# One reading transfer per tile, an earlier place for four pieces of the weights, and three groups of sums on GpSimd in a Fourier mixing and ELU kernel

## The chip, the cores and the metric

The kernel runs on one core of one Trainium2 chip. The metric is the device time of a whole execution in microseconds; the time before is the median of 3 runs. The core has a matrix engine (TensorE, PE in the profile, its weight loads PEld), a vector engine (VectorE, DVE), an activation engine (ScalarE, ACT), GpSimd (POOL) and SyncE (SP), which here only issues transfers. Each engine runs its own queue strictly in the order of the program; engines wait for one another through semaphores.

## The reference

```python
# x: (8, 3008, 256); filt_r, filt_i: (1505, 256), float32; w_in: (256, 2048); w_out: (2048, 256), float64
X = np.fft.rfft(x, axis=1)
y = np.fft.irfft(X * (filt_r + 1j * filt_i)[None], n=3008, axis=1).astype(np.float32)
h = y.reshape(24064, 256) @ w_in
g = np.where(h > 0, h, np.exp(np.minimum(h, 0)) - 1.0)
out = (g @ w_out).astype(np.float32)
```

The weights arrive as 8-byte floats (`moe_w_in`, `moe_w_out` are read as pairs of 32-bit words) and have to be turned into 4-byte floats on the core.

## The kernel before, in words

**Three factors of the Fourier step.** A sequence of 3008 = 47 x 64 rows is transformed by three small matrix factors. The first factor works on rows 47 apart (`a_first` for the first batch, `a_unit` for the other seven). The second factor, with the filter's product and the way back, goes over groups g of four frequencies (`b_first`, `products`, `bi_first` for batch 0; `b_unit`, `re_mult`, `im_mult`, `bi_unit` for the others). Its result goes to a DRAM buffer `yds[b]` of 32 x 96 rows of 256 floats (`y_write_first`, `y_write`). The third factor (`n_unit`) reads it back in six parts m: `y_read` brings a tile of 128 partitions x 4 rows (512 KB), and `n_unit` multiplies it with a table `tn` of 128 x 128 per row, which yields the transposed input y of the two large products. The partition p*32+k of that tile holds part p (0 to 3) of frequency k (0 to 31), so one read is four transfers of 32 partitions; the first read (`y_read_first`) is eight, because the last four frequencies are written last and are read apart.

**The two large products.** For each of the 48 tiles (b, m) there are four quads q, each a seven-product Strassen form of `y @ w_in` (ups, with the tiles phs, pha, phd in PSUM), the ELU, and the seven products with `w_out` (downs, tiles po). The item i runs the ups of quad i and the downs of quad i-1, so quad q of the first tile needs `w_in[q]`, and one quad later `w_out[q]`. `n_sums` makes the three combinations of y which the seven products need. In the first tile a seven-product step is 4 matmuls of 224 columns, in the later ones of 256 columns.

**The weights.** `w_in` and `w_out` are cut into 16 pieces k = 4q + j: pieces with j = 0, 1 are the two halves of `w_in[q]`, those with j = 2, 3 the two halves of `w_out[q]`. Each piece goes through `w_fetch` (a transfer of 512 KB), `w_split` (two operations on VectorE), `w_float` (four on ScalarE, parts 0 to 3), `w_join` (on VectorE: sign and exponent, mantissa sum, then the product that lands in `w_in[q]` or `w_out[q]`), and after the second piece of a pair `w_sums` (four additions of 128 x 256 floats on VectorE, for the combined weights of the seven products). Six sets of temporaries (`wtmp`) hold pieces between split and join.

**The order.** The program is written out by hand (`tc.manual_schedule`). A boot part does the first factor of batch 0, pieces 0 to 6, then the loop over g of the second factor (lines 868 to 883) with some floats in between (`floats`), then the first read, pieces 7 to 13 in part, seven idle matmuls (`warm`), and `n_unit(0, 0)`. After it comes the loop over items (line 976). In it a table `plan` holds what else is issued in a quad, under (quad, place): place 2 is behind the third of the quad's first seven or eight steps, place 0 behind all of these, place 1 at the quad's end. In the first quads the plan has the rest of the weights and the start of batch 1: `x_unit` and `a_unit` in quads 2, 3 and 4 (they also issue `x_load` and `z_write`), `f_pairs` in quads 1 to 4 (DRAM to DRAM transfers for the filter), `z_read` in quad 5 and `b_unit` in quad 6. SyncE issues nearly all transfers, in program order, and waits in that order too.

The lines in question: `y_read` 472, `y_read_first` 477, `w_split` 709, `w_float` 715, `w_join` 724, `w_sums` 745, the loop of the second factor 865 to 883, the boot's end 884 to 897, the plan's list 920 to 925, the items 976 to 998. In the profile the additions of `w_sums` have lines 749 to 752, the operations of `w_join` 728, 730 and 735 or 741, those of `w_split` 712 and 713, of `w_float` 722; 627 is a down product, 545 an up product, 494 the third factor's, 233 the first factor's of batch 1.

Of the kernel before, what the change touches and what calls it, by code (L numbers as in the profile page):

```python
# [11 lines left out]
FP32 = mybir.dt.float32  # L12
U32 = mybir.dt.uint32
AXT = mybir.ActivationFunctionType
ALU = mybir.AluOpType
# [11 lines left out]
P = 128  # L27
D = 256
B = 8
DFF = 2048  # L30
H = 24
K2 = 32
# [9 lines left out]
def _make_tables():  # L42

    n2, k2 = np.arange(N2), np.arange(K2)
    ta, tn = np.zeros((P, H, P)), np.zeros((P, H, P))
    for i in range(H):
        for h in range(2):
            if h and i == 0:
                continue  # L60
            n1 = N1 - i if h else i
            th = 2 * np.pi * (((N1 * n2[:, None] + n1) * k2[None]) % N) / N
            c, s = np.cos(th), -np.sin(th)
            c[:, 0], s[:, 0] = 1.0, 1.0 - 2.0 * (n2 % 2)
# [12 lines left out]
    c, s = np.cos(th), np.sin(th)  # L77
    sign = np.where(q < 24, 1.0, -1.0)
    gb[0:24, 0, :N1], gb[24:48, 0, :N1] = c, s
    gb[64:88, 0, :N1], gb[88:112, 0, :N1] = c * sign, -s * sign  # L80
    for o in (0, 64):
        gr[o:o + N1, 0, 0:24], gr[o:o + N1, 0, 24:48] = 2 / N * c.T, 2 / N * s.T
        gi[o:o + N1, 0, 0:24], gi[o:o + N1, 0, 24:48] = 2 / N * (c * sign).T, -2 / N * (s * sign).T
    k1 = np.arange(24)[None]
    t0 = 2 * np.pi * ((i * k1) % N1) / N1
    t3 = 2 * np.pi * ((i * (32 + 64 * k1)) % N) / N
    c0, s0, c3, s3 = np.cos(t0), np.sin(t0), np.cos(t3), np.sin(t3)
    gb[0:24, 1, 0:24], gb[24:48, 1, 24:48] = c0, c3
    gb[64:88, 1, 24:48], gb[88:112, 1, 0:24] = -s3, -s0

    m0, m3 = np.full((24, 1), 2 / N), np.full((24, 1), 2 / N)
    m0[0] = m3[23] = 1 / N
    s0[:, 0] = s3[:, 23] = 0.0
    gr[0:24, 1, 0:24], gr[24:48, 1, 24:48] = m0 * c0.T, m3 * c3.T
    gi[0:24, 1, 24:48], gi[24:48, 1, 0:24] = -m0 * s0.T, -m3 * s3.T

    fb, bb = np.zeros((P, 2, 32)), np.zeros((P, 2, 4, 32))
    for p in range(4):  # L100
        r = slice(32 * p, 32 * p + 24)
        fb[r, 0, :24] = (-1.0 if p == 3 else 1.0) * gb[24 * (p % 2):24 * (p % 2) + 24, 0, 0:24]
        q = (0, 24, 64, 88)[p]
        k = 24 if p in (1, 2) else 0
        fb[r, 1, :24] = gb[q:q + 24, 1, k:k + 24]
    for o in range(0, P, 32):
        for p, (t, c) in enumerate(((gr, 0), (gr, 24), (gi, 0), (gi, 24))):
            bb[o:o + 24, 0, p, :24] = t[0:24, 0, c:c + 24]

    bb[0:24, 1, 0, :24], bb[0:24, 1, 1, :24] = gr[0:24, 1, 0:24], gr[24:48, 1, 24:48]  # L110
    bb[0:24, 1, 2, :24], bb[0:24, 1, 3, :24] = gi[24:48, 1, 0:24], gi[0:24, 1, 24:48]
    pairs = np.concatenate([fb.reshape(P, 64), bb.reshape(P, 2 * P)], 1)
    lie = np.concatenate([2 * np.arange(24), 2 * np.arange(24) + 1])
    gb[:, :, lie] = gb[:, :, :48].copy()
    for t in (gr, gi):
        for o in (0, 64):
            t[o + lie] = t[o:o + 48].copy()
    gf = np.zeros_like(gb)
    for o in (0, 64):
        gf[o:o + 48] = gb[o:o + 48].reshape(2, H, 2, 64).swapaxes(0, 1).reshape(48, 2, 64)  # L120
    once = np.stack([np.eye(P), gf.reshape(P, P)], 1)
    return [t.astype(np.float32) for t in (ta, tn, np.stack([gb, gr, gi], 1), tf, once, pairs)]

# [7 lines left out]
def kernel(  # L131
# [9 lines left out]
    nc = tc.nc  # L141
# [18 lines left out]
    t4p = pool("t4p", 2)  # L160
# [308 lines left out]
        w = tns[b, m] = tnp.tile([P, 4, P], FP32, tag="tn", name="tn")  # L469
        nc.sync.dma_start(w, tn_d[:, 4 * m:4 * m + 4, :])  # L470

    def y_read(b, m, queues=(nc.sync, nc.sync)):
        t = t4s[b, m] = t4p.tile([P, 4, D], FP32, tag="t4", name="t4")
        for p in range(4):
            queues[p % 2].dma_start(t[p * 32:p * 32 + 32, :, :], yds[b][:, p * H + 4 * m:p * H + 4 * m + 4, :])

    def y_read_first():
        t = t4s[0, 0] = t4p.tile([P, 4, D], FP32, tag="t4", name="t4")
        for k in (slice(0, K2 - 4), slice(K2 - 4, K2)):
            for p in range(4):  # L480
                nc.sync.dma_start(t[p * 32 + k.start:p * 32 + k.stop, :, :], yds[0][k, p * H:p * H + 4, :])

    def half(m):

# [197 lines left out]
    wds = {}  # L682
# [24 lines left out]
    wts, wtmp = {}, []  # L707

    def w_split(k):
        m, e, f, l = wts[k] = wtmp[{9: 2, 12: 3, 13: 4, 15: 5}.get(k, k % 2)]  # L710
        hi = wds[k][:, :, 1]
        nc.vector.tensor_scalar(out=m, in0=hi, scalar1=0x000FFFFF, scalar2=None, op0=ALU.bitwise_and)
        nc.vector.tensor_scalar(out=e, in0=hi, scalar1=0x7FF00000, scalar2=None, op0=ALU.bitwise_and)
# [7 lines left out]
            o, x, func, scale, bias = steps[i]  # L721
            nc.scalar.activation(out=o, in_=x, func=func, scale=scale, bias=bias)  # L722

    def w_join(k):
        q, j = divmod(k, 4)
        m, e, f, l = wts.pop(k)
        hi = wds.pop(k)[:, :, 1]
        nc.vector.scalar_tensor_tensor(out=e, in0=hi, scalar=0x80000000, in1=e,
                                       op0=ALU.bitwise_and, op1=ALU.bitwise_or)
        nc.vector.tensor_tensor(out=f, in0=f, in1=l, op=ALU.add)  # L730
        e = e.bitcast(FP32)
        if j < 2:
            f, e = (t.rearrange("p (a j c) -> p a j c", a=2, j=2) for t in (f, e))
# [8 lines left out]
        if j % 2 == 1 and k < 7:  # L742
            w_sums(k)

    def w_sums(k):
        q, j = divmod(k, 4)
        w = (w_in if j < 2 else w_out)[q]
        a11, a21, a12, a22, s1, s2, s4 = (w[:, i] for i in range(7))
        nc.vector.tensor_tensor(out=s1, in0=a21, in1=a22, op=ALU.add)
        nc.vector.tensor_tensor(out=s2, in0=s1, in1=a11, op=ALU.subtract)  # L750
        nc.vector.tensor_tensor(out=s4, in0=a12, in1=s2, op=ALU.subtract)
        nc.vector.tensor_tensor(out=a21, in0=a11, in1=a21, op=ALU.subtract)

    def f_arrange():

# [27 lines left out]
    with tc.manual_schedule():  # L783


        with tc.tile_pool(name="boot", bufs=1) as bp:
# [75 lines left out]
            w_split(7)  # L862
            w_join(6)
            w_split(8)
            floats = {0: (7, 0, 1), 1: (7, 2, 3), 4: (8, 0, 1), 5: (8, 2, 3), 6: (9, 0, 1), 7: (9, 2, 3)}
            for g in range(4):
                t_first(g)
            for g in range(NG + 2):
# [10 lines left out]
                    w_float(*floats[g])  # L879
                if g == 1:  # L880
                    w_split(9)
                if 3 <= g < 6:
                    w_fetch(g + 8, nc.sync)
            y_read_first()
            for k in (14, 15):
                w_fetch(k, nc.sync)
            for k in (7, 8):
                w_join(k)
                w_split(18 - k)
                w_float(18 - k)  # L890
            for k in (12, 13):
                w_split(k)
                w_float(k)
            w_sums(7)
            w_join(9)
            w_sums(9)
            w_join(10)
            warm = psO.tile([P, 512], FP32, tag="po2", name="warm")
            for k in range(7):
                nc.tensor.matmul(warm, w_in[0][:, 0, 0, :], w_in[0][:, 0:2].rearrange("p a b c -> p (a b c)"),  # L900
# [15 lines left out]
        def at(quad, place, fn, *a):  # L916
            plan.setdefault((quad, place), []).append((fn, a))


        for quad, place, fn, *a in ((0, 0, w_split, 14), (1, 2, w_join, 11), (1, 2, w_split, 15), (1, 2, w_float, 14, 0, 1),  # L920
                                    (1, 1, w_float, 14, 2), (2, 2, w_sums, 11), (2, 2, w_float, 14, 3),
                                    (2, 2, w_float, 15, 0), (2, 1, w_join, 13), (2, 1, w_sums, 13), (2, 1, w_float, 15, 1),
                                    (3, 2, w_float, 15, 2, 3), (3, 1, w_join, 14), (3, 1, w_join, 15),
                                    (4, 2, w_sums, 15)):
            at(quad, place, fn, *a)
        for c in range(2, XBUFS):
            at(c - 2, 0, x_load, 1, c)
# [6 lines left out]
        for b in range(B):  # L934
# [28 lines left out]
            for m, (s, place) in enumerate(((23, 0), (25, 1), (29, 1), (32, 0), (36, 0), (40, 0))):  # L963
# [4 lines left out]

                    at(*((t + s + 1, 1) if m > 2 else (t + s, place)), n_sums, b, m)
                if b == 0 and m == 1:  # L970
                    at(1, 1, w_join, 12)
                at(t + PER + 4 * m + 5, 0, c_unit, b, m)
                at(t + PER + 4 * m + 6, 0, o_unit, b, m)

# [1 line left out]
        for i in range(-PER, len(items) + 3):  # L976
# [3 lines left out]
            for n, k in enumerate("DUUDUDDU" if i in opens else "UUDUDDU"):  # L980
                s = ups if k == "U" else downs
                if s:
                    s.pop(0)()
                if n == 2:
                    for fn, a in plan.get((i, 2), ()):
                        fn(*a)
            for fn, a in plan.get((i, 0), ()):
                fn(*a)
# [42 lines left out]
```

## Time and profile before

| | us |
|---|---|
| median of 3 runs | 2598.8 (2598.58 to 2601.48) |
| the profiled execution | 2598.4 |
| its span | 2596.6 |
| TensorE busy in the span | 2549.5 |
| VectorE busy | 2042.1 |
| ScalarE busy | 1548.0 |
| GpSimd busy | 159.0 |
| mean granted clock of TensorE, as a share of full speed | 0.995 |

The profile is of one execution. Its time is 1.8 us over its span, for what lies ahead of the first and behind the last instruction. Starts are in us from the span's start. In a timeline a row gives start, duration, engine, line, operation, operands and shape, a count, and in brackets how long the engine sat idle before it and what released it. A busy share says little of the path: what counts is where TensorE, which is busy nearly all the time, stands still, and which wait ends last there. Transfers that are issued by SyncE show when they are issued, and seldom when they land. A transfer's tile can bear the name of another tensor that shares its memory: the wait of the third factor at 84.5 us is said to be for `t<-in_moe_w_out_dram`, and the program has `y_read_first` there.

### The profile page before, as it was taken

How to read it: one execution, taken by the hardware profiler on the slowest of the kernel's cores; microseconds unless marked ns; L12 is line 12 of the kernel's file. 1: busy time of each engine (PE TensorE's matmuls, PEld its weight loads, DVE VectorE, ACT ScalarE, POOL GpSimd, SP SyncE). 2: the span in 40 equal slices, each digit the busy share in tenths (PEclk: the TensorE clock that was granted, in tenths of full speed). 3: DMA queues.
4: the chain of work that ended last, by engine and by line, in shares of the span. 5: the costliest groups of instructions: out<-in, count | busy, mean ns of one | idle time of the engine just before them, and what ended most of it. 6: DMA issues, size and time to landing. Idle time of an engine off the chain costs nothing.

```text
span 2596.6 us, 39712 instructions
## 1 busy us (share of the span) xinstructions
PE 2549.5 (98%) x14474; PEld 2203.3 (85%) x14474; DVE 2042.1 (79%) x3536; ACT 1548.0 (60%) x2713; POOL 159.0 (6%) x313
## 2 busy tenths in 40 slices
PE   6889999999999999999999999999999999999998
PEld 4778889888898888988889888888889888898887
DVE  6968887788877888788886888778887788866666
ACT  6755655666556655665566655566555655555554
POOL 4000100010000000000000000000000011000000
PEclk9999999999999999999999999999999999999999
DMA  9663213522234231433215231343213322110010
GB/s 286 180 162 76 70 27 94 130 70 58 52 91 119 60 76 47 116 82 76 63 41 146 70 84 37 78 121 85 59 44 85 91 59 69 43 43 20 21 29 17
DMA packets 231475, 206.37 MB, mean 79 GB/s; under 512 B 130962, under 2 KB 197714, under 8 KB 231280
## 3 DMA queue, kind: packets, MB, share of 16 engines
q1 hardware_dynamic: 215920, 172.95, 27.1%
q0 software_dynamic: 14000, 30.44, 4.2%
q8 instruction: 114, 1.87, 0.3%
q10 hardware_dynamic: 1360, 0.46, 0.1%
q14 instruction: 81, 0.66, 0.1%
HBM read 131.87 MB, written 78.17 MB: 81 GB/s over the span
## 4 chain that ended last, share of the span: by engine, by line
PE 96%; DMA 2%; DVE 1%; ACT 1%; issue 0%; SPq 0%; DVEq 0%; ACTq 0%
PE po L627 44%; PE phs L545 25%; PE phd L545 12%; PE pha L545 6%; PE psn L494 3%; PE psa L233 1%; PE pf L382 1%; PE pv L454 1%; DMA t<-in_moe_w_in_dram 1%; DMA wd<-in_moe_w_out_dram 0%; DMA xc<-in_x_dram 0%; DMA yd<-t 0%; PE po L295 0%; PE po L329 0%; PE psr L329 0%
## 5 line engine op out<-in xcount | busy, mean ns | idle before, releaser
L627 PE MATMUL po<-g,wo 128*128 128x256 f32 (+1 forms) x5376 | 1314.7, 376 | 6.9 <-DVE wo L741 4.8
L627 PEld LDWEIGHTS po<-g,wo 128*128 128x128 f32 x5376 | 1012.9, 190 | 171.1 <-issue 49.4
L556 ACT ACTIVATE g<-phs 128x512 f32<-128x512 f32 (+1 forms) x576 | 339.0, 589 | 762.2 <-PE phs L545 760.8
L563 ACT ACTIVATE e<-e 128x512 f32<-128x512 f32 (+1 forms) x768 | 477.2, 621 | 24.4
L553 DVE TENSOR_TENSOR g<-phd,g 128x512 f32<-128x512 f32 (+1 forms) x384 | 259.4, 676 | 295.1 <-ACT e L563 204.1
L545 PE MATMUL phs<-ys,wi 128*128 128x256 f32 (+1 forms) x1536 | 388.5, 375 | 1.5 <-ACT g L556 1.5
L545 PE MATMUL phs<-y,wi 128*128 128x256 f32 (+1 forms) x1536 | 388.6, 375 | 0.0
L567 DVE SCALAR_TENSOR_TENSOR g<-e,g 128x512 f32<-128x512 f32 (+1 forms) x576 | 387.0, 672 | 0.3 <-ACT e L563 0.2
L562 ACT ACTIVATE e<-g 128x512 f32<-128x512 f32 (+1 forms) x576 | 353.4, 614 | 44.3 <-DVE g L553 37.1
L545 PEld LDWEIGHTS phs<-ys,wi 128*128 128x128 f32 x1536 | 292.0, 190 | 35.5 <-ACT g L556 2.2
L545 PEld LDWEIGHTS phs<-y,wi 128*128 128x128 f32 x1536 | 288.2, 190 | 36.1 <-ACT r L387 0.4
L567 DVE SCALAR_TENSOR_TENSOR g<-e,phs 128x512 f32<-128x512 f32 (+1 forms) x192 | 129.8, 676 | 141.3 <-ACT e L563 140.9
L545 PE MATMUL phd<-ys,wi 128*128 128x256 f32 (+1 forms) x768 | 195.3, 377 | 1.7 <-DVE g L553 1.7
L545 PE MATMUL pha<-y,wi 128*128 128x256 f32 (+1 forms) x768 | 194.4, 376 | 1.2 <-ACT t L722 1.2
L545 PE MATMUL phd<-y,wi 128*128 128x256 f32 (+1 forms) x768 | 193.7, 375 | 0.0
L562 ACT ACTIVATE e<-phs 128x512 f32<-128x512 f32 (+1 forms) x192 | 113.0, 589 | 128.8 <-PE phs L545 128.8
L545 PEld LDWEIGHTS phd<-ys,wi 128*128 128x128 f32 x768 | 144.5, 190 | 22.6 <-DVE g L553 6.8
L545 PEld LDWEIGHTS pha<-y,wi 128*128 128x128 f32 x768 | 145.5, 191 | 19.2 <-ACT t L722 1.5
L545 PEld LDWEIGHTS phd<-y,wi 128*128 128x128 f32 x768 | 145.8, 190 | 16.5
L323 POOL DMA_DIRECT2D fall<-fp x224 | 110.4, 501 | 732.2 <-DVE r L427 704.5
L553 DVE TENSOR_TENSOR g<-pha,g 128x512 f32<-128x512 f32 (+1 forms) x192 | 129.1, 672 | 27.0 <-PE pha L545 26.9
L607 DVE TENSOR_TENSOR g<-g,g 128x512 f32<-128x512 f32 (+1 forms) x192 | 130.7, 681 | 6.7
(159 smaller groups left out, 2085.8 us busy)
## 6 DMA issues: line engine op xcount, KB each, us to landing
yd<-t SPq DMA_DIRECT2D x127, 192.0 KB
t<-yd SPq DMA_DIRECT2D x188, 128.0 KB
z<-t SPq DMA_DIRECT2D x84, 256.0 KB
fall<-fp POOLq DMA_DIRECT2D x224, 96.0 KB, 2.9
t<-z SPq DMA_DIRECT2D x224, 96.0 KB
out_dram<-o SPq DMA_DIRECT2D x632, 32.0 KB
tn<-tn_t SPq DMA_DIRECT2D x48, 256.0 KB
xc<-in_x_dram SPq DMA_DIRECT2D x84, 128.0 KB
```

What stands on the lines that cost most here:

```text
L233: nc.tensor.matmul(p[o:o + 64, u, :], w[r, u, o:o + 64], src[r, u, :], start=True, stop=True)
L323: nc.gpsimd.dma_start(t[32 * a:32 * a + 24].rearrange("p c u d -> p (c u d)"), fp[g, a].rearrange("q c u d -> q (c u d)"))
L382: nc.tensor.matmul(pf[p][1][32 * a:32 * a + 32, js, :], fb[r, v, :], t2[r, js, a, :], start=True, stop=True, tile_position=(32 * p, 32 * a))
L494: nc.tensor.matmul(ps[:, ts(q, P)], t[:, i - 4 * m, ds(dh * P, P)], w[:, i - 4 * m, :], start=True, stop=True)
L545: nc.tensor.matmul(ps[:, a, 0:h], w_in[q][:, COMBO[n], a, :], y[n], start=start and a == 0, stop=True, skip_group_check=True)
L553: nc.vector.tensor_tensor(out=g[o], in0=i0, in1=i1, op=ALU.add)
L556: nc.scalar.activation(out=g[o], in_=i0, func=AXT.Copy)
L562: nc.scalar.activation(out=e, in_=src, func=AXT.Relu, scale=-1.0)
L563: nc.scalar.activation(out=e, in_=e, func=AXT.Exp, scale=-1.0)
L567: nc.vector.scalar_tensor_tensor(out=g[n], in0=es[n], scalar=1.0, in1=src, op0=ALU.subtract, op1=ALU.max)
L607: nc.vector.tensor_tensor(out=g["t4"], in0=g["b21"], in1=g["t2"], op=ALU.subtract)
L627: nc.tensor.matmul(po[i][:, u, 0:h], w_out[q][:, COMBO[n], a, :], g[n][:, a, :], start=q == 0 and a == 0 and n in (1, 3, 6, 4), stop=True, ...
```

## The change

**The read.** The partition of the third factor's tile becomes 4k+p instead of p*32+k: the table `tn` is rearranged on the host for that, and the source is seen as `(k p)` rows, so that one transfer covers all 128 partitions. The first read becomes two transfers, of 112 and of 16 partitions; `y_read_first` is gone.

**The boot.** In the loop over g, the floats of pieces 8, 9 and 10 come at g = 2 to 7 (before: 8 and 9 at g = 4 to 7), `w_join(7)` comes at g = 2 with the sums 7 on GpSimd, and `w_split(10)` at g = 5. Behind the loop VectorE has `w_join(8)`, the splits of 11, 12 and 13, `w_join(9)`, the sums 9, `w_join(10)` and now `w_join(11)`; the sums 11 go to GpSimd. The temporaries of 10 and 11 swap.

**The quads.** A place 3 is added, behind the fifth step. In quad 1, `w_join(12)` stands where `w_join(11)` was and `w_join(13)` where `w_join(12)` was, with the sums 13 on GpSimd. Piece 14 is joined in two parts in quad 2 and piece 15 behind it (before: both at the end of quad 3), and the sums 15 are made in quad 3 (before: in quad 4). The floats of 14 and 15 move to places 2 and 3 of quads 1 and 2.

```diff
+    tn = np.ascontiguousarray(tn.reshape(4, K2, H, P).swapaxes(0, 1)).reshape(P, H, P)
...
-    def y_read(b, m, queues=(nc.sync, nc.sync)):
+    def y_read(b, m, *parts):
         t = t4s[b, m] = t4p.tile([P, 4, D], FP32, tag="t4", name="t4")
-        for p in range(4):
-            queues[p % 2].dma_start(t[p * 32:p * 32 + 32, :, :], yds[b][:, p * H + 4 * m:p * H + 4 * m + 4, :])
-
-    def y_read_first():
-        t = t4s[0, 0] = t4p.tile([P, 4, D], FP32, tag="t4", name="t4")
-        for k in (slice(0, K2 - 4), slice(K2 - 4, K2)):
-            for p in range(4):
-                nc.sync.dma_start(t[p * 32 + k.start:p * 32 + k.stop, :, :], yds[0][k, p * H:p * H + 4, :])
+        for k in parts or (slice(0, K2),):
+            r = slice(4 * k.start, 4 * k.stop)
+            nc.sync.dma_start(t[r], yds[b].rearrange("k (p i) d -> (k p) i d", p=4)[r, 4 * m:4 * m + 4, :])
...
-        m, e, f, l = wts[k] = wtmp[{9: 2, 12: 3, 13: 4, 15: 5}.get(k, k % 2)]
+        m, e, f, l = wts[k] = wtmp[{9: 2, 10: 1, 11: 0, 12: 3, 13: 4, 15: 5}.get(k, k % 2)]
...
-    def w_sums(k):
+    def w_sums(k, engine=nc.vector, parts=(0, 1, 2, 3)):
...
-            floats = {0: (7, 0, 1), 1: (7, 2, 3), 4: (8, 0, 1), 5: (8, 2, 3), 6: (9, 0, 1), 7: (9, 2, 3)}
+            floats = {0: (7, 0, 1), 1: (7, 2, 3), 2: (8, 0, 1), 3: (8, 2, 3), 4: (9, 0, 1), 5: (9, 2, 3), 6: (10, 0, 1), 7: (10, 2, 3)}
...
+                if g == 2:
+                    w_join(7)
+                    w_sums(7, nc.gpsimd)
+                if g == 5:
+                    w_split(10)
...
-            y_read_first()
+            y_read(0, 0, slice(0, K2 - 4), slice(K2 - 4, K2))
...
-            for k in (7, 8):
-                w_join(k)
-                w_split(18 - k)
-                w_float(18 - k)
-            for k in (12, 13):
+            w_join(8)
+            for k in (11, 12, 13):
                 w_split(k)
                 w_float(k)
-            w_sums(7)
             w_join(9)
             w_sums(9)
             w_join(10)
+            w_join(11)
+            w_sums(11, nc.gpsimd)
...
-        for quad, place, fn, *a in ((0, 0, w_split, 14), (1, 2, w_join, 11), (1, 2, w_split, 15), (1, 2, w_float, 14, 0, 1),
-                                    (1, 1, w_float, 14, 2), (2, 2, w_sums, 11), (2, 2, w_float, 14, 3),
-                                    (2, 2, w_float, 15, 0), (2, 1, w_join, 13), (2, 1, w_sums, 13), (2, 1, w_float, 15, 1),
-                                    (3, 2, w_float, 15, 2, 3), (3, 1, w_join, 14), (3, 1, w_join, 15),
-                                    (4, 2, w_sums, 15)):
+        for quad, place, fn, *a in ((0, 0, w_split, 14), (1, 2, w_join, 12), (1, 2, w_split, 15), (1, 2, w_float, 14, 0, 1),
+                                    (1, 3, w_float, 14, 2, 3), (2, 2, w_float, 15, 0, 1), (2, 3, w_float, 15, 2, 3),
+                                    (2, 0, w_join, 14, (0,)), (2, 1, w_join, 14, (1,)), (2, 1, w_join, 15),
+                                    (3, 0, w_sums, 15, nc.vector, (0, 1, 2)), (3, 1, w_sums, 15, nc.vector, (3,))):
...
-                    at(1, 1, w_join, 12)
+                    at(1, 1, w_join, 13)
+                    at(1, 1, w_sums, 13, nc.gpsimd)
...
-                if n == 2:
-                    for fn, a in plan.get((i, 2), ()):
+                if n in (2, 4):
+                    for fn, a in plan.get((i, 2 + n // 4), ()):
                         fn(*a)
```

More of the change, by code (lines that the diff above doesn't have):

```diff
@@ L722, in w_float, with w_join @@
             nc.scalar.activation(out=o, in_=x, func=func, scale=scale, bias=bias)
-    def w_join(k):
+    def w_join(k, parts=(0, 1)):
         q, j = divmod(k, 4)
[L726 to L730, printed above, removed]
+        m, e, f, l = wts[k]
+        if 0 in parts:
+            nc.vector.scalar_tensor_tensor(out=e, in0=wds.pop(k)[:, :, 1], scalar=0x80000000, in1=e,
+                                           op0=ALU.bitwise_and, op1=ALU.bitwise_or)
+            nc.vector.tensor_tensor(out=f, in0=f, in1=l, op=ALU.add)
+        if 1 not in parts:
+            return
         e = e.bitcast(FP32)
@@ L748, in w_sums @@
         a11, a21, a12, a22, s1, s2, s4 = (w[:, i] for i in range(7))
[L749 to L752, printed above, removed]
+        sums = ((s1, a21, a22, ALU.add), (s2, s1, a11, ALU.subtract), (s4, a12, s2, ALU.subtract), (a21, a11, a21, ALU.subtract))
+        for i in parts:
+            o, x, y, op = sums[i]
+            engine.tensor_tensor(out=o, in0=x, in1=y, op=op)
     def f_arrange():
```

## The prediction

> **What bounds the kernel now.** The page comes first: TensorE is busy 98% of the span. So only its idle time, and the time it runs at half clock, can be won. The table of stretches shows where these lie.
>
> ```profile
> PE 2549.5 (98%) x14474; PEld 2203.3 (85%) x14474; DVE 2042.1 (79%) x3536; ACT 1548.0 (60%) x2713; POOL 159.0 (6%) x313
> ...
> core 0: us, PE busy (x) PEld busy (x) DVE busy (x) ACT busy (x) POOL busy (x), PEclk, DMA share, GB/s
> 67.00:88.00 21.00, 18.34 (x106) 10.52 (x101) 20.39 (x42) 18.31 (x32) 0.00 (x0) 0.92 0.83 238
> 98.00:122.70 24.70, 22.97 (x149) 21.58 (x149) 23.34 (x45) 16.61 (x31) 1.90 (x2) 1.00 0.40 106
> 122.70:136.80 14.10, 12.88 (x92) 11.54 (x88) 11.46 (x22) 9.13 (x18) 0.52 (x1) 1.00 0.75 202
> 136.80:159.30 22.50, 15.63 (x64) 12.97 (x64) 12.85 (x25) 7.83 (x15) 0.53 (x1) 0.85 0.73 192
> 159.30:187.30 28.00, 28.00 (x167) 24.07 (x171) 19.84 (x38) 16.99 (x31) 3.45 (x7) 1.00 0.58 146
> 187.30:2480.00 2292.70, 2292.68 (x13082) 1989.42 (x13083) 1831.11 (x3148) 1366.18 (x2394) 121.89 (x242) 1.00 0.29 72
> ```
>
> From 159.3 to 2480 us TensorE never stops; nothing in the change shortens that. The last stretch before it, quad 4, holds 22.5 us, and its 14 steps need only 7 x 0.757 (four matmuls of 224 columns) + 7 x 0.865 (of 256) = 11.35. The waits of TensorE from 80 to 200 us say why:
>
> ```profile
> PE po L627 <- DVE wo L741: 4.8, 2, 3.4
> PE psn L494 <- DMA t<-in_moe_w_out_dram: 2.7, 1, 2.7
> PE po L627 <- DVE wo L751: 2.1, 1, 2.1
> PE phd L545 <- DVE g L553: 1.7, 1, 1.7
> PE pha L545 <- ACT t L722: 1.2, 1, 1.2
> ```
>
> L741 is the join of pieces 14 and 15, L751 their sums: 6.9 us of quad 4. VectorE is late there because it ran all but unbroken from 95 to 130 us. The timeline has the joins at quad 3's end:
>
> ```profile
> 138.50 0.68 DVE L728 SCALAR_TENSOR_TENSOR we<-t,we 128x512 uint32<-128x512 uint32 x1
> 139.10 0.68 DVE L730 TENSOR_TENSOR wfl<-wfl 128x512 f32<-128x512 f32 x1
> 139.81 0.76 DVE L741 TENSOR_TENSOR wo<-wfl,we 128x256 f32<-128x256 f32 x2
> ```
>
> Each long stall also costs clock. In half-microsecond stretches the granted clock falls at about 84.4, 142.3 and 149.1 us, for 3.4 us each:
>
> ```profile
> 84.00:84.50 0.50, 0.00 (x0) 0.02 (x1) 0.47 (x2) 0.50 (x1) 0.00 (x0) 0.79 0.98 365
> ...
> 85.00:85.50 0.50, 0.50 (x5) 0.50 (x4) 0.50 (x3) 0.50 (x2) 0.00 (x0) 0.50 0.64 160
> ```
>
> **The change, part by part.** Starts in the rows give the price per operation: join of a `w_out` piece 2.0 us (73.57 to 75.57), of a `w_in` piece 1.93, split 0.67, a group of sums 1.59 (80.18 to 81.77), four floats 2.45.
>
> (1) Loop of the second factor. VectorE gets `w_join(7)`, 2.0 us. It falls into a gap of 2.21 (57.4 to 59.63), in which the product of g = 3 waits for TensorE: cost nothing. `w_split(10)`, 0.67, falls where VectorE has no gap (66 to 73.6) and delays the last products by 0.3 to 0.7; ScalarE's copies behind them start at 75.55 in any case, so the last write leaves 0.1 to 0.4 later; I take 0.2. The floats of 8 fill ScalarE gaps of 2.18 and 1.80 (at 57.5 and 61.8); from g = 4 on ScalarE has as many floats as before.
>
> (2) Boot's end. The last write lands at 80.78, now 81.0; then four transfers were issued (to 82.05) and the data was there at 84.51, 2.46 later. One issue of 0.3 gives 81.3 + 2.46 = 83.7. `warm` ends at 81.85, so TensorE idles some 1.9 instead of 2.66. ScalarE has three pieces to float behind the write instead of four: free at 84.55 instead of 86.98. At full clock the third factor's two halves take 0.95 each (1.95 for both at 106.33), so the second copy ends at 86.1, against 88.63: -2.5. At half clock, as now, it ends near 87.8: -0.8. The nearest case is the wait of 1.73 before 118.33, after which the clock stayed full; I take -2.5. VectorE: join 8, three splits, join 9, sums 9, joins 10 and 11 are 11.5 us from 73.9, so it is ready at 85.45, ahead of the copies.
>
> The Trainium skill ("TensorE: Matmul & The Clock Gate", Part 1) says that the clock halves after an idle window of about 3.4 us. Here 2.66 us of idleness were enough, and the measurement decides; by the page the clock would have stayed full before as well, and -0.8 would be the right term.
>
> (3) Sums on GpSimd. No row shows a two-input addition there. The nearest is its copy of 32 x 256, 0.39 us at best, and 1.26 for two where VectorE works beside it (the short addition on VectorE taking 0.61 instead of 0.42):
>
> ```profile
> 534.48 1.26 POOL L440 COPY zs<-r 32x256 f32<-32x256 f32 x2 [6.69 <-DVE zs L437]
> ...
> 534.87 0.61 DVE L643 TENSOR_TENSOR k<-k,c 128x256 f32<-128x256 f32 x1
> ```
>
> So four additions last 1.6 us at the least; doubled for the second input 3.2, and some 5 with waits. Nobody needs them within that: sums 7 (at 59.4) are used in quad 2, sums 11 (at 85.5) in quad 3, sums 13 (at about 110) in quad 3. The cost is what VectorE loses: 0.07 (0.2 on one addition, less what a gap hides) to 0.7 (one whole addition) per operation that meets one of two SBUF inputs. Sums 7 meet products from PSUM: nothing. Sums 11 meet the four of `n_sums`: +0.1 to +1.8, taken 0.6. Sums 13 meet `w_join(14)` and `x_unit`: +0.15 to +2.8, taken 0.9. GpSimd's clearing of the batch 1 tile (57.22 now) falls behind sums 11, to 89; if SyncE waits for it at 85, its later reads are 4 us late, against 10 us between `y_read(0, 1)` (issued by 93.6) and its use at 106.3: nothing.
>
> The Trainium skill ("SBUF — State Buffer", Who interferes with whom) speaks against this part: a VectorE instruction with two SBUF inputs and a GpSimd one that reads SBUF exclude each other for their whole length. "GPSIMD Engine Reference" (Elementwise) has additions 1.96 times as long there; an estimate by both pages is 4 x 0.42 x 1.96 = 3.3 us lost per group, 6.6 in all, where I put 1.5.
>
> (4) Quads 1 and 2 on VectorE: join 12 for 11 and join 13 for 12 save 0.07 each; in quad 2 the sums 11 (1.59) go and the first half of join 14 (1.2) comes, ahead of `x_unit` and the addition that TensorE waits for at 117.66: -0.5. That stall of 1.73 so stays, starting -2.5 + 0.6 - 0.5 + 0.9 = -1.5 us earlier. The moved floats (1.37 us each) fall into ScalarE gaps of 1.73 in quads 1 and 2.
>
> (5) Quad 3: no float stands before the matmul that waited 1.22 for one: -1.2 (bounds 0 and -1.22). VectorE: its quad 2 tail ends at 123.5 - 1.5 = 122.0, the rest of joins 14 and 15 (2.7) at 124.7, then one addition (0.54), sums 15 (1.25) and `x_unit` (2.65): 129.2, where TensorE asks at 131.8 - 2.7 = 129.1. Just covered; each us more is a stall.
>
> (6) Quad 4: nothing is left to join. 22.45 (136.82 to 159.26) becomes 11.35: -11.1; with 1.6 us of new small waits -9.5.
>
> (7) SyncE. From 122.0 (it waits for batch 1's first products) to 155.97 it issues without a wait for TensorE, 34 us, then 11.5 us from 160.39 (a wait for quad 4's products), 2.6 for landing, and eight `z_read` to 178.07. Now it starts at 120.5, `y_read` saves 1.36, and quad 4's products are long there: 120.5 + 32.6 + 11.5 + 2.6 + 3.5 = 170.7, landed 2.46 later at 173.2. `b_unit` at 187.30 will be reached at 187.3 - 13.8 = 173.5. So 7 us of slack shrink to nearly none: 0 to +3, taken 0.5.
>
> The other 47 reads: issued 1.36 us shorter on a queue that TensorE doesn't wait for (192.54, used at 207.29): nothing.
>
> Sum: -2.5 + 0.6 - 0.5 + 0.9 - 1.2 - 11.1 + 0.5 = -13.3. The profiled execution took 2598.4 (span 2596.6 and 1.8 around it; the median is 2598.8): **2585.1 us**. All best ends give -2.5 + 0.1 - 0.5 + 0.15 - 1.22 - 11.1 + 0 = -15.1 (2583.3); all worst -0.8 + 1.8 - 0.5 + 2.8 + 0 - 9.5 + 3 = -3.2 (2595.2).
>
> **Rivals.**
> A, SyncE's chain takes the stall over. If transfers squeezed together issue more slowly (SyncE's rows have 0.9 to 1.65 us for pairs where traffic is dense), `z_read` lands 3 to 6 us later and the gain is 10.3 to 7.3: about 2588.5 to 2591.5. For it: the slack in (7). Against: traffic between 111 and 122 is nil.
> B, the change doesn't do what it says: the chain does not move at all. Landed at 180.6 as now, it leaves 187.3 - 180.6 = 6.7; with the joins of 14 and 15 also late in quad 3 for the two clock windows (1.7 each), 3.3 are left: 2595, within what can be told from no change. Against: only one of SyncE's waits there is for something that stays in place.
> C, slower: one read of 512 KB lands later than the last of four of 128 KB, and `n_unit` stalls. Over 47 reads it decides from (13.3 + 5.2) / 47 = 0.39 us each; at 0.6 it is 2598.4 - 13.3 + 28 = 2613. Such a read has 14.7 us to land, and 512 KB on GpSimd's queue took 7.3 from issue to landing in the list of transfers: much against it.
>
> **How the numbers follow.** A difference of 0.2%, 5.2 us, is about what a measurement of this kernel can tell from no change. Main case 0.65 (2582.5 to 2588.5, its own range); A 0.14; B 0.09; C 0.09; a larger gain than all best ends 0.03. Faster is the main case, A and the larger gain: 0.82; same 0.09, slower 0.09. The range takes the main case, A, and the worst sum's better part: 2582.5 to 2593.
>
> **What would show it.** TensorE's waits for L741 and L751 in quad 4 gone, and no half clock near 140 (6); the third factor's wait at 84 under 2 us and its first matmuls at full clock (2); VectorE's short additions near 86 and 111 at 0.4 to 0.8 (3); TensorE's wait for L553 near 116 still 1 to 3 us (4); `b_unit`'s first matmul near 174 without a wait for `z_read` (7). Wrong: a new wait in quad 3 for L553 of over 3 us, a wait at `b_unit` of over 3 us, or waits of `psn` after 200 us.

## The result, and the profile after

The changed kernel takes 2592.9 us (median of 9 runs, 2589.8 to 2596.5) against 2599.2 us for the kernel before in the same series: a ratio of 0.9976, with a 95% interval of 0.9966 to 0.9986. So it is faster by 6.2 us (3.6 to 8.8), where 13.3 us had been worked out. The profiled execution took 2593.7 us with a span of 2591.9; against the profiled execution before that is 4.7 us, and the ledger below is made against this.

The busy line of the page hardly differs from before. GpSimd has 10 us more, TensorE has 2.2 us more and did the same work: it ran longer at half clock.

```profile
PE 2551.7 (98%) x14474; PEld 2204.0 (85%) x14474; DVE 2041.2 (79%) x3524; ACT 1548.1 (60%) x2713; POOL 169.1 (7%) x325
```

The table of stretches, cut at the ends of the same quads as before, shows what was won and lost (length, then busy time of the engines, then the granted clock; the rows are quad 2 with what lies ahead of it in quad 1, quad 3, quad 4, the way to `b_unit`, `b_unit`, and the rest):

```profile
97.60:126.60 29.00, 25.94 (x148) 23.60 (x148) 26.88 (x48) 18.20 (x33) 5.75 (x6) 0.88 0.38 103
126.60:139.30 12.70, 12.70 (x92) 11.64 (x88) 9.75 (x20) 7.87 (x16) 0.52 (x1) 1.00 0.71 188
139.30:150.90 11.60, 11.60 (x64) 10.58 (x60) 7.67 (x14) 7.75 (x15) 0.54 (x1) 1.00 0.73 210
150.90:178.90 28.00, 28.00 (x161) 24.03 (x160) 19.94 (x38) 16.99 (x31) 3.47 (x7) 1.00 0.77 209
178.90:190.00 11.10, 10.98 (x65) 6.75 (x65) 7.86 (x13) 4.84 (x10) 0.00 (x0) 0.85 0.34 71
190.00:2480.00 2290.00, 2290.00 (x13040) 1988.05 (x13039) 1827.63 (x3141) 1365.08 (x2391) 121.88 (x242) 1.00 0.28 72
```

Quad 4 is down from 22.5 us to 11.6 and quad 3 from 14.1 to 12.7, both now without an idle moment of TensorE. But the stretch of quad 2 grew from 24.7 to 29.0 us at a clock of 0.88, and `b_unit`'s has a clock of 0.85. The waits of TensorE from 60 to 200 us:

```profile
PE phd L541 <- DVE g L549: 3.1, 1, 3.1
PE psn L490 <- DMA t<-yd: 2.1, 1, 2.1
PE phs L541 <- ACT g L552: 1.5, 2, 0.9
PE phs L541 <- DVE ys L518: 0.4, 1, 0.4
```

The joins and sums of pieces 14 and 15 are gone from the list. The wait in quad 2 (L541 for L549, which were 545 and 553 before) has grown from 1.73 to 3.06 us. TensorE's timeline there shows what it drags along: the four matmuls behind the wait take 1.86 us instead of 1.02, and the clock is back only at `psa`.

```profile
115.38 0.92 PE L623 MATMUL po<-g,wo 128*128 128x224 f32 x4
119.36 1.86 PE L541 MATMUL phd<-ys,wi 128*128 128x224 f32 x4 [3.06 <-DVE g L549]
121.02 3.19 PE L623 MATMUL po<-g,wo 128*128 128x224 f32 x8
```

The timeline at `b_unit` (L383): its 40 matmuls last 4.34 us where they lasted 1.72 before. TensorE's weight loads wait inside them for the `z_read` transfers, and half clock follows from 183.5 to 186.9 us.

```profile
178.91 4.34 PE L383 MATMUL pf<-t,pairs 24*32 24x256 f32 x40
183.18 1.82 PE L623 MATMUL po<-g,wo 128*128 128x256 f32 x4
184.79 1.91 PE L541 MATMUL phs<-y,wi 128*128 128x256 f32 x4
```

The ledger in us against the profiled execution before (each row is the change over that stage, read from the starts of the same instruction in both traces):

| stage | forecast | profile after | missing |
|---|---|---|---|
| ahead of the changed part: second factor's first matmul (46.92 to 47.89) | 0 | +1.0 | 1.0 |
| from there to the end of the second copy of y (41.71 to 39.81) | -2.5 | -1.9 | 0.6 |
| sums 11 beside `n_sums` (next down step in quad 0) | +0.6 | +0.6 | 0 |
| quads 1 and 2, to the end of `psa` (122.68 to 126.64) | +0.4 | +4.3 | 3.9 |
| quad 3 (14.14 to 12.68) | -1.2 | -1.5 | -0.3 |
| quad 4 (22.44 to 11.54) | -11.1 | -10.9 | 0.2 |
| to `b_unit` and from there to the end | +0.5 | +3.7 | 3.2 |
| sum | -13.3 | -4.7 | 8.6 |

Two places therefore owe most: 3.9 us in quad 2 and 3.2 us at `b_unit`. The first row is chance: nothing that was changed lies ahead of that matmul, and from 40 to 45 us the granted clock was 0.65 in this execution, 1.00 in the one before. Over the ten profiles of this document the matmul starts anywhere from 46.82 to 51.59 us, and the execution before is at the early end. A ledger between two executions is therefore good for places, and the medians for the sum: by these 7.1 us are missing, not 8.6.

### The profile page after: what moved, and what is told of

Same layout as the page of the kernel before. It is cut to its first block, busy times and chain, and to the rows that moved or that the text cites. A ratio compares the mean times of both kernels' runs of the same rounds, so it can differ in the third digit from the quotient of the medians.

```text
span 2591.9 us, 39471 instructions
## 1 busy us (share of the span) xinstructions
PE 2551.7 (98%) x14474; PEld 2204.0 (85%) x14474; DVE 2041.2 (79%) x3524; ACT 1548.1 (60%) x2713; POOL 169.1 (7%) x325
## 3 DMA queue, kind: packets, MB, share of 16 engines
q8 instruction: 114, 1.87, 0.3%
## 4 chain that ended last, share of the span: by engine, by line
PE 96%; DMA 2%; DVE 1%; ACT 0%; issue 0%; SPq 0%; DVEq 0%; ACTq 0%
PE po L623 44%; PE phs L541 25%; PE phd L541 13%; PE pha L541 6%; PE psn L490 3%; PE psa L234 2%; PE pf L383 2%; PE pv L455 1%; DMA xc<-in_x_dram 1%; DMA x<-in_x_dram 0%; PE po L330 0%; DMA yd<-t 0%; PE po L296 0%; PE psr L330 0%; DMA t<-yd 0%
## 5 line engine op out<-in xcount | busy, mean ns | idle before, releaser
L549 DVE TENSOR_TENSOR g<-phd,g 128x512 f32<-128x512 f32 (+1 forms) x384 | 259.6, 676 | 293.6 <-ACT e L559 205.1
L541 PE MATMUL phs<-ys,wi 128*128 128x256 f32 (+1 forms) x1536 | 387.6, 375 | 2.0 <-ACT g L552 1.5
L541 PE MATMUL phs<-y,wi 128*128 128x256 f32 (+1 forms) x1536 | 388.5, 375 | 0.0
L541 PEld LDWEIGHTS phs<-ys,wi 128*128 128x128 f32 x1536 | 291.4, 190 | 36.0 <-ACT g L552 3.0
L541 PEld LDWEIGHTS phs<-y,wi 128*128 128x128 f32 x1536 | 288.2, 190 | 35.8 <-ACT g L552 0.2
L541 PE MATMUL phd<-ys,wi 128*128 128x256 f32 (+1 forms) x768 | 196.2, 378 | 3.1 <-DVE g L549 3.1
L541 PE MATMUL pha<-y,wi 128*128 128x256 f32 (+1 forms) x768 | 194.0, 375 | 0.0
L541 PE MATMUL phd<-y,wi 128*128 128x256 f32 (+1 forms) x768 | 193.7, 375 | 0.0
L541 PEld LDWEIGHTS phd<-ys,wi 128*128 128x128 f32 x768 | 145.0, 191 | 24.1 <-DVE g L549 8.2
L541 PEld LDWEIGHTS pha<-y,wi 128*128 128x128 f32 x768 | 145.6, 190 | 17.5 <-ACT y L492 0.2
L541 PEld LDWEIGHTS phd<-y,wi 128*128 128x128 f32 x768 | 145.8, 190 | 16.5
L549 DVE TENSOR_TENSOR g<-pha,g 128x512 f32<-128x512 f32 (+1 forms) x192 | 129.3, 673 | 25.9 <-PE pha L541 25.7
```

What stands on the lines that cost most here:

```text
L541: nc.tensor.matmul(ps[:, a, 0:h], w_in[q][:, COMBO[n], a, :], y[n], start=start and a == 0, stop=True, skip_group_check=True)
L549: nc.vector.tensor_tensor(out=g[o], in0=i0, in1=i1, op=ALU.add)
```

## The theories and the experiments

**The first theory** is that quad 2 is the cause of both. GpSimd's sums 13 run from 112.77 to 116.90, in front of the one addition (L549) that TensorE waits for, and VectorE's operations beside them get longer. VectorE's timeline of the changed kernel has it (0.68 is the undisturbed duration):

```profile
113.05 1.00 DVE L724 SCALAR_TENSOR_TENSOR we<-t,we 128x512 uint32<-128x512 uint32 x1
113.97 1.21 DVE L726 TENSOR_TENSOR wfl<-wfl 128x512 f32<-128x512 f32 x1
115.10 1.21 DVE L220 TENSOR_TENSOR sd<-xc 128x512 f32<-128x512 f32 x1
116.35 1.10 DVE L221 TENSOR_TENSOR xc<-xc 128x512 f32<-128x512 f32 x1
...
118.69 0.62 DVE L549 TENSOR_TENSOR g<-phd,g 128x448 f32<-128x448 f32 x1
```

GpSimd's own rows (start, duration of all four):

```profile
59.80 3.04 POOL L750 TENSOR_TENSOR wo<-wo 128x256 f32<-128x256 f32 x4 [2.48 <-DVE wo L739]
86.42 3.22 POOL L750 TENSOR_TENSOR wo<-wo 128x256 f32<-128x256 f32 x4 [23.58 <-DVE wo L739]
112.77 4.13 POOL L750 TENSOR_TENSOR wi<-wi 128x256 f32<-128x256 f32 x4 [22.55 <-DVE wi L733]
```

SyncE waits for `psa` and starts batch 1's transfers at 125.97 instead of 122.00, so by this theory `z_read` is late as well. The runs bear out the first half of the theory and not this second one.

**The rival** is SyncE's chain: that it is too long by itself (rival A of the prediction), so that the stall at `b_unit` would stay, whatever quad 2 does. A third question is what the new read is worth. The kernel before took 2600.7 us (median of 13) beside the first four experiments and 2600.5 (of 22) beside the others; the ratios are to these.

### Sums 13 elsewhere, and on another engine in the same place

The first experiment moves sums 13 from GpSimd to VectorE, and from quad 1's end to quad 2's end, behind the critical addition:

```diff
-                                    (2, 0, w_join, 14, (0,)), (2, 1, w_join, 14, (1,)), (2, 1, w_join, 15),
+                                    (2, 0, w_join, 14, (0,)), (2, 1, w_sums, 13), (2, 1, w_join, 14, (1,)), (2, 1, w_join, 15),
...
-                    at(1, 1, w_sums, 13, nc.gpsimd)
```

> Theory 1: the sums 13 on GpSimd stretched the four VectorE operations that stand ahead of the addition TensorE waits for in quad 2 (4.3 us for four, 2.5 without company); that made the wait for L549 3.1 us instead of 1.7 and halved the clock behind it for 6.8 us. With these sums on VectorE at quad 2's end the four operations take 2.5 again, the wait is 0.8 to 1.7, the clock stays full there, quad 4 ends 4 to 5 us earlier than with the change (near 146.5), and the time is 2585 to 2589. Theory 2 (SyncE's chain of transfers to z_read is the bound, whatever VectorE does): quad 4 ends earlier too, but the first product of batch 1 (line 383) waits by as much longer, and the time stays at 2591 to 2594.

Measured: 2589.9 us (5 runs, 2586.5 to 2590.3), ratio 0.9955 (0.9943 to 0.9968): 10.8 us faster than the kernel before, 4.6 us more than the change brought, though 0.9 above the expected range. The interval just touches the changed kernel's (0.9966 to 0.9986), so the rows have to carry the cause. Its profiled execution has a span of 2584.7. VectorE's timeline at the same operations, now undisturbed:

```profile
112.93 0.68 DVE L724 SCALAR_TENSOR_TENSOR we<-t,we 128x512 uint32<-128x512 uint32 x1
113.53 0.69 DVE L726 TENSOR_TENSOR wfl<-wfl 128x512 f32<-128x512 f32 x1
114.13 0.69 DVE L220 TENSOR_TENSOR sd<-xc 128x512 f32<-128x512 f32 x1
114.85 0.69 DVE L221 TENSOR_TENSOR xc<-xc 128x512 f32<-128x512 f32 x1
...
116.79 0.62 DVE L549 TENSOR_TENSOR g<-phd,g 128x448 f32<-128x448 f32 x1
```

From the first of these to the addition it is 3.86 us, where the changed kernel has 5.64: sums 13 on GpSimd cost VectorE 1.78 us. TensorE's timeline of this kernel:

```profile
117.46 1.02 PE L541 MATMUL phd<-ys,wi 128*128 128x224 f32 x4 [1.29 <-DVE g L549]
118.32 1.68 PE L623 MATMUL po<-g,wo 128*128 128x224 f32 x8
...
175.22 1.72 PE L383 MATMUL pf<-t,pairs 24*32 24x256 f32 x40
```

The wait is 1.29 us instead of 3.06, the clock stays full, and `b_unit` (the last row) runs in 1.72 us without a stall. A part returned in quad 3, where VectorE now has the sums: a wait of 0.87 us.

The second experiment separates the engine from the place: sums 13 where the changed kernel has them, but on VectorE.

```diff
-                    at(1, 1, w_sums, 13, nc.gpsimd)
+                    at(1, 1, w_sums, 13)
```

> The same sums on VectorE at their place at quad 1's end. Theory 1: 1.6 us of additions take the place of 1.8 us of stretching, all of it ahead of the addition that TensorE waits for: the wait for L549 is 2.5 to 3.3 us, and the time that of the changed kernel, 2591 to 2594. If GpSimd's company costs more than the stretching that the rows show, the time is below 2590.

Measured: 2593.0 us (9 runs, 2587.4 to 2600.1), ratio 0.9969 (0.9959 to 0.9979). The changed kernel's interval overlaps with it: no difference can be told. The profiled execution is the longest of its series (2600.1), with a boot that ended 3.5 us later, so only its local rows are used. VectorE's timeline (the last row is the addition that TensorE waits for) and TensorE's waits:

```profile
118.11 1.68 DVE L750 TENSOR_TENSOR wi<-wi 128x256 f32<-128x256 f32 x4
119.71 0.62 DVE L549 TENSOR_TENSOR g<-pha,g 128x448 f32<-128x448 f32 x1
120.25 0.68 DVE L724 SCALAR_TENSOR_TENSOR we<-t,we 128x512 uint32<-128x512 uint32 x1
...
124.11 0.62 DVE L549 TENSOR_TENSOR g<-phd,g 128x448 f32<-128x448 f32 x1
```

```profile
PE phd L541 <- DVE g L549: 3.0, 1, 3.0
```

On VectorE the four sums take 1.68 us themselves, the work behind them is undisturbed again (3.86 us from 120.25 to 124.11), and the wait is 3.0 us. GpSimd, which lengthens VectorE's work by 1.78 us, takes nothing off it here. What the first experiment mended is the place, not the engine.

The Trainium skill ("SBUF — State Buffer", Who interferes with whom) says that a VectorE instruction with two SBUF inputs and a GpSimd instruction that reads SBUF exclude each other for the whole length of one. In these runs the four operations that met became longer by 0.32 to 0.53 us each and none stood still for long; the estimate from the pages was 3.3 us lost per group, the measured loss is 1.78, for sums 11 it is 1.14 (below). The direction of the rule held, and the price was about half to a third of its worst reading.

### SyncE's chain shortened

`f_pairs` (the transfers for the filter, which SyncE issues) all go to quads 1 and 2, away from SyncE's way from quad 2 to `z_read`; first alone, then together with the late sums 13.

```diff
-                at(1 + 2 * c + u, 0, f_pairs, c, u)
+                at(1 + c, 0, f_pairs, c, u)
```

> The filter's transfers of quads 3 and 4 move to quad 2, where SyncE waits 15 us for batch 1's first products. Theory 1: quad 2 stays as it is (wait of 3 us, half clock), but SyncE's way to z_read is 7 to 9 us shorter, so the first product of batch 1 takes 1.7 instead of 4.3 us and no half clock follows (1.7): 2588 to 2590. Theory 2: the same here, 2588 to 2590. If the 4.3 us have another cause than z_read, 2592 to 2594.

> Both edits. Theory 1, in which SyncE's lateness is mostly a consequence of quad 2: nearly the time of the kernel with the late sums alone, 2584 to 2588. Theory 2: the gain of the early filter transfers and that of the late sums come only together: 2584 to 2587, while the late sums alone stay at 2591 or more.

Measured: alone 2591.6 us (5 runs, 2588.7 to 2592.8), ratio 0.9963 (0.9951 to 0.9976); together 2588.7 us (5 runs, 2586.8 to 2590.5), ratio 0.9953 (0.9941 to 0.9966). With the early `f_pairs` alone, `z_read` is issued at 170.84 and `b_unit` at 179.90 has its 1.72 us: the stall there is gone, although the wait of 3.07 us in quad 2 remains.

```profile
121.89 1.86 PE L541 MATMUL phd<-ys,wi 128*128 128x224 f32 x4 [3.07 <-DVE g L549]
...
179.90 1.72 PE L383 MATMUL pf<-t,pairs 24*32 24x256 f32 x40
```

So the transfers do end the stall, but that brings little: by the medians' ratios some 3 us alone, with an interval that overlaps the changed kernel's, and 1.2 us on top of the late sums, which is within the spread. Both medians lie above the expected ranges, by 1.6 and 0.7 us. With both edits 12.0 us of the forecast 13.3 are there. In the first experiment the stall had gone as well, without this edit: TensorE then took 53.4 us from the end of quad 2's `psa` to `b_unit`, with the wait of 0.87 us in quad 3, against 52.3 in the changed kernel, and SyncE 51.7 us from its start to the last `z_read` against 53.0. So it was just in time there by a slower TensorE and a faster SyncE together.

### The change once more, the read alone, and the joins back

The changed kernel again (a second profile); the kernel before with the merged reads and the new table alone; and the changed kernel with joins 14 and 15 and sums 15 where they were before:

```diff
-                                    (2, 0, w_join, 14, (0,)), (2, 1, w_join, 14, (1,)), (2, 1, w_join, 15),
-                                    (3, 0, w_sums, 15, nc.vector, (0, 1, 2)), (3, 1, w_sums, 15, nc.vector, (3,))):
+                                    (3, 1, w_join, 14), (3, 1, w_join, 15),
+                                    (4, 2, w_sums, 15)):
```

> The changed kernel itself, beside the other runs of this call: 5 to 9 us under the kernel before (it was 6.2 under), and quad 2 as in its first profile: the four operations ahead of the addition 5.6 us from the first's start to the addition's, the wait for L549 3 us, half clock behind it. Theory 1 and theory 2 expect the same.

> The kernel before with the reads by one transfer alone. The prediction's term: the first read's data 0.8 us earlier, so -0.8 to -2.7 with the clock, and nothing at the other 47 reads: 1 to 3 us under the kernel before. The rival that the profiles after suggest: the transfer of 112 partitions waits for the last write of both halves (it was issued 2 us later) and takes longer, so the data is there 7.3 to 8.5 us after the last copy, as before (7.9): 0 to 1 us, not to be told from no change.

> The changed kernel with the joins of 14 and 15 at quad 3's end again and the sums 15 in quad 4. The prediction's step 6 has 11.1 us for these: TensorE waits for L739 (4 to 5 us) and for L750 (2 us) in quad 4 with one or two windows of half clock, so quad 4 takes 20 to 22.5 us instead of 11.5; quad 2 is 1.2 us better, and the first product of batch 1 waits less. Time 2 to 6 us above the changed kernel. Rival: SyncE's chain holds the end anyway, then no more than 1 us above it.

Measured, the change again: 2592.6 us (6 runs, 2589.5 to 2596.7), ratio 0.9973 (0.9961 to 0.9985), the first result once more. Its TensorE timeline:

```profile
120.59 1.02 PE L541 MATMUL phd<-ys,wi 128*128 128x224 f32 x4 [3.07 <-DVE g L549]
121.45 1.68 PE L623 MATMUL po<-g,wo 128*128 128x224 f32 x8
...
177.20 4.28 PE L383 MATMUL pf<-t,pairs 24*32 24x256 f32 x40
181.41 2.08 PE L623 MATMUL po<-g,wo 128*128 128x256 f32 x4
```

The wait is the same to 0.01 us, and yet the clock stays full behind it. This execution's span is 2589.8, 2.1 us shorter, although its third factor started 0.9 later (85.97). The stall at `b_unit` is there again, as long as before (4.28 less 1.72), with half clock behind it. So the half clock of quad 2 is not what makes it. SyncE and TensorE both go on from the same `psa`, and a later `psa` moves both; what counts is how long SyncE then takes to its last `z_read`. Its first and last rows, in the changed kernel's first profile and in this one:

```profile
125.97 0.36 SPq L203 DMA_DIRECT2D ta<-ta_t  x1
175.76 3.17 SPq L314 DMA_DIRECT2D t<-z  x8
```

```profile
124.26 0.35 SPq L203 DMA_DIRECT2D ta<-ta_t  x1
174.34 3.18 SPq L314 DMA_DIRECT2D t<-z  x8
```

That is 53.0 and 53.3 us, and 53.6 in the second experiment, where `b_unit` stalls for 3.0 us.

Measured, the read alone: 2599.9 us (11 runs, 2598.9 to 2601.1), ratio 0.9998 (0.9990 to 1.0007): no gain, with bounds of -2.6 and +1.8 us. SyncE's rows of the two boots, before and here (eight transfers, then two; the last write was issued by ScalarE at 76.66 and 79.44):

```profile
78.38 3.66 SPq L481 DMA_DIRECT2D t<-yd  x8
```

```profile
82.36 1.48 SPq L477 DMA_DIRECT2D t<-yd  x2
```

Counted from the issue of the last write, the last read's issue ends at 5.4 us before and at 4.4 us here, so the expected 0.8 us was saved on SyncE. But the data is there at 7.9 us before (84.51) and at 7.7 us here (87.16): from the last issue to the data it is 2.5 us before, 3.3 us here and 3.0 us in the changed kernel. Of the old eight, four were out between 78.38 and 80.5, while the writes of the last group were still landing; the single transfer of 112 partitions goes out only 1.2 us ahead of the small one. That its 448 KB are what lands late is argued from this; the trace does not say which of the two ended last.

Measured, the joins back: 2597.1 us (11 runs, 2595.1 to 2599.9), ratio 0.9988 (0.9979 to 0.9997); 4.5 us slower than the changed kernel beside it. TensorE's waits:

```profile
PE po L623 <- DVE wo L739: 4.6, 2, 3.4
PE po L623 <- DVE wo L750: 2.1, 1, 2.1
PE psn L490 <- DMA t<-yd: 1.9, 1, 1.9
PE phd L541 <- DVE g L549: 1.7, 1, 1.7
```

The waits of quad 4 are back to within 0.2 us (4.6 + 2.1 where before had 4.8 + 2.1), with a clock of 0.72 from 140 to 152 us. But the wait in quad 2 falls to 1.7 us, since the half join of 14 (1.20 us, from 112.93 to 114.13 in the first experiment) is no longer ahead of the addition. So the early joins win the 6.7 us of quad 4's waits and the clock lost there, and pay for it at the very place where sums 13 stand.

### Both mended

The last experiment takes everything off the critical addition that can stand elsewhere: sums 13 late, `f_pairs` early, sums 11 on VectorE in quad 0, and joins 14 and sums 15 each in one piece behind the quad's critical work.

```diff
-            w_sums(11, nc.gpsimd)
...
+        for quad, place, fn, *a in ((0, 0, w_split, 14), (0, 0, w_sums, 11), (1, 2, w_join, 12), (1, 2, w_split, 15), (1, 2, w_float, 14, 0, 1),
...
+                                    (2, 1, w_sums, 13), (2, 1, w_join, 14), (2, 1, w_join, 15),
+                                    (3, 1, w_sums, 15)):
...
-                at(1 + 2 * c + u, 0, f_pairs, c, u)
+                at(1 + c, 0, f_pairs, c, u)
...
-                    at(1, 1, w_sums, 13, nc.gpsimd)
```

> The early filter transfers and the late sums 13, and besides: sums 11 on VectorE in quad 0 (where it waits 1.6 us for a product), piece 14 joined whole at quad 2's end, sums 15 whole at quad 3's end. Theory 1 (what VectorE has ahead of the two additions that TensorE waits for in quads 2 and 3 is what is left): the waits for L549, 1.29 and 0.87, fall to 0.1 and 0 to 0.9, n_sums is 1 us shorter; 1 to 3 us under the kernel with both edits, near 12 to 15 us under the kernel before. If the work only moves the wait: quad 3 waits 1 to 2 us and the time is that of the kernel with both edits.

Measured: 2588.0 us (5 runs, 2585.3 to 2588.6), ratio 0.9949 (0.9936 to 0.9961): 12.5 us faster than the kernel before, and the fastest of all. TensorE's waits from 60 to 200 us:

```profile
PE psn L490 <- DMA t<-yd: 2.6, 1, 2.6
PE phs L541 <- ACT g L552: 1.5, 2, 0.9
PE phd L541 <- DVE g L549: 0.9, 1, 0.9
PE po L623 <- DVE wo L750: 0.2, 1, 0.2
```

Quad 2 has no wait for the addition left that this list shows (the 0.9 us are in quad 3), and `b_unit` starts at 174.88 and has its 1.72 us. Of GpSimd's three groups only sums 7, in the boot, is left. Against the first experiment, and against the kernel with both edits, the intervals overlap: that this version is better than these is likely by its median, and not shown. The 0.7 us that it gains on both edits by the medians are less than the 1 to 3 us expected.

## Why the prediction was partly wrong

By the medians 6.2 us came of the 13.3. What is missing lies in two places: the wait and the clock at the end of quad 2 (steps 3 and 4), and SyncE's chain up to `b_unit` (step 7).

**What was right.** Quad 4 (step 6) gave 10.9 us of the forecast 11.1, quad 3 (step 5) 1.5 of 1.2, and both stages run without a wait. The joins put back confirm it. The second factor's loop (step 1) cost nothing: from its first matmul to the end of ScalarE's last copy it is 29.7 us in both profiles (46.92 to 76.64, 47.89 to 77.58), with join 7 in its gap from 57.6 to 59.7 and sums 7 on GpSimd behind it. The sums 11 of step 3 were taken at 0.6; the four operations of `n_sums` grew from 0.39 each to 0.50, 0.49, 0.91 and 0.80 us, 1.14 together, of which 0.6 reached TensorE. No wait for the other 47 reads appears (rival C falls: nothing after 200 us waits for `psn`), and the chain did move (rival B falls, although the time came near to it).

**Step 3 failed in size, and step 4 in what hangs on it.** Sums 13 were taken at 0.9 us, with a bound of 2.8; they cost 1.78. With -0.4 for the half join in place of sums 11, that makes a wait of 3.06 us, where step 4 has the stall of 1.73 "stay". The 2.9 us of half clock behind it are in no term: from the wait's end to the end of `psa` it is 7.28 us, against 4.36 in the first experiment. The prediction had written that each long stall costs clock, and then summed delays at a stall that existed already as if they were delays alone. By its own list the sign to look for there was a wait of 1 to 3 us; it should have priced what the upper end does to the clock. That price varies: from the wait's end to the end of `psa` it is 7.3 us again in the second experiment, 5.75 with the early `f_pairs`, and 4.35 in the second profile of the changed kernel, at waits of 3.01 to 3.07 us.

**Step 7 was right for TensorE and too short for SyncE.** It worked out a slack of "nearly none" and took 0.5 of 0 to 3. TensorE reaches `b_unit` 52.9 us after SyncE's start (125.97 to 178.91), where the step had 53.0 (120.5 to 173.5). But SyncE needs 53.0 us to the end of its last `z_read`, where the step added up 50.2: 1.0 more for its 32.6, 1.3 more for its 11.5, 0.6 more for the landing of 2.6, and 0.3 less for `z_read` itself. These 2.8 us make the stall (4.34 less 1.72, which is 2.6); the half clock behind it makes the loss 4.3 by the third factor's next matmuls near 203 us. Of this 0.6 come back by the end of the execution, from where was not traced, so that the ledger has 3.7, 3.2 more than forecast. So rival A's place and size were right (SyncE late by about 3 us), beside the gain of quad 4 and not in its stead. Whether dense traffic lengthened the chain, as A has it, no run shows apart: single rows grew, such as a pair of `z_write` at 148.16, which took 3.66 us with a wait of 2.4 in it instead of 1.3, and in the second profile others.

**Step 2 held two terms, and neither is sure.** Of its 2.5 us, 0.8 was for the issue saved; the rest was for the clock. The issue: the data came 3.0 us after the last issue instead of the 2.46 taken over from before. Over eight executions with the changed boot, from the end of ScalarE's last copy to the third factor's first matmul it was 7.3 to 8.5 us (mean 7.8), against 7.87 before, so this part is near nothing. The clock: in the profiled execution it was full, and the third factor took 2.02 us where it had taken 3.55. But of the eight executions five had 2.02 and three ran a part of it at half clock (3.06 to 3.43 us), so that 1.0 to 1.4 us come in some executions and not in others.

**The clock as a matter of chance.** Step 2 argued by one neighbouring case (a wait of 1.73 that kept the clock). The runs show why one case is not enough: of waits of 3.06 and 3.07 at the same instruction of the same kernel, one halved the clock for 6.8 us and the other did not; the same wait of 3.07 with the early `f_pairs` halved it for 3.4, one of 3.01 in the second experiment for 6.8. Before the third factor, idle times of 1.87, 2.15, 2.56, 2.61 and 3.09 us kept the clock, and 1.87, 2.05, 2.66, 2.83 and 2.95 in other executions did not. The Trainium skill ("TensorE: Matmul & The Clock Gate", Part 1) has the gate look at a free-running window of about 3.4 us, and that agrees with the lengths here: half clock lasted 3.4 us each time, or twice that in quad 2 (118.7 to 125.5). Where the idle time falls in such a window would explain why like waits end differently; the traces do not show the windows while the clock is full, so this is not shown. The page's other sentence, that the clock falls after a whole idle window, does not agree: in quad 2 TensorE had worked until 116.3 and the clock fell at 118.7. For a forecast such a wait has a chance and a price (in quad 2 nothing, 1.4, 2.9 and 2.9 us in four executions), not one answer.

**What stays open.** Why the data of the merged read lands later behind its last issue was not tried apart, nor what makes SyncE's chain to `z_read` vary from 51.7 to 53.6 us at the same program order of its transfers. Sums 13 on GpSimd at a later time were not tried either: GpSimd is idle and starts as soon as join 13 has landed (the row at 112.77 gives that as its release), so a later place in the program would not move them.

## What to carry to other kernels

Price work that is moved to another engine by what stands beside it: GpSimd's four additions cost VectorE as much as doing them itself (1.78 against 1.68 us), and TensorE paid for it because they ran in front of the one operation that it waited for; ask of every moved piece which critical operation is the next on each engine that it disturbs. Add a clock price to a stall that already exists before you lengthen it. Where a chain of transfers is left with no slack by the sum, take its length with a margin: here it came out 2.8 us over 50.2 and made a second stall. Merging transfers saved issues and not latency here; that the merged transfer starts later than the first of the parts did is the likely reason, and not shown.

## What the runs showed of the hardware

Two-input additions of 128x256 floats on GpSimd took 0.76 us each (3.04 for four) beside VectorE operations with one input in PSUM, which kept their 0.68 us. Beside VectorE operations with two SBUF inputs they took 0.81 and 1.03 in the mean of a group, and where it was 1.03 the VectorE operations of 128x512 went from 0.68 to between 1.00 and 1.21 us: both slow down. The same addition takes 0.42 us on VectorE. At the end of quad 2 the clock stayed at half for a second 3.4 us, though TensorE had worked through four fifths of the first (from 119.36 in 118.7 to 122.1). With the early `f_pairs` it had worked from 121.89 in 121.3 to 124.8, a little more, and the clock came back after the first.
